# RWKV-7 attention with a mixture of experts on one core: from the ninth unit on, K and B are turned to channels on VectorE

## The chip, the cores and the metric

The kernel runs on one core of a Trainium2 chip. A core has TensorE (PE; its weight loads are listed as PEld), VectorE (DVE), ScalarE (ACT), GpSimd (POOL) and SyncE (SP), which here only issues DMAs. Each engine works through its own instructions in order and waits at semaphores for the others. The metric is device time in microseconds (us) of one execution; of several runs, the median.

## The reference

Attention over 4 batches, 8 heads, 768 tokens and a head dimension of 40, with a state that decays channel by channel, and then four expert networks, weighted per token:

```python
for t in range(S):                                     # attention, S = 768
    kt, vt, rt = (k[:, :, t], v[:, :, t], r[:, :, t])
    wt, at, bt = (w[:, :, t], a[:, :, t], b[:, :, t])
    y[:, :, t] = np.einsum('bhd,bhde->bhe', rt, state)
    Sa = np.einsum('bhde,bhe->bhd', state, at)
    state_decay = state * wt[:, :, None, :] - np.einsum('bhd,bhe->bhde', Sa, bt)
    state = state_decay + np.einsum('bhd,bhe->bhde', vt, kt)
...
p = domain_probs / (domain_probs.sum(-1, keepdims=True) + 1e-09)
for e in range(E):                                     # mixture, E = 4, F = 1024
    h = np.maximum(x @ w1[e], 0.0)
    out += p[:, e:e + 1] * (h @ w2[e])
```

All data is float32.

## The kernel before

**Units and passes.** The 768 tokens are cut into 12 chunks of 64, and the 4 batches into 2 pairs. A unit is one chunk of one pair: 24 units, `u = 2 * chunk + pair`. The main loop (L1221) makes a pass for each unit. In pass u the generator `within` (L462) prepares unit u + 2, `substitute` (L638) solves its triangular system, `merge` (L704) joins the two halves of the solution of unit u + 1, and `step` (L742) brings the state forward by a unit. Between these parts, pieces of the mixture (`mix`, L1088) of earlier chunks fill TensorE. From unit 7 on (`q.apart`) the order is always the same.

**Layouts.** "By channels" is a tile with channels on the partitions: 128 partitions are two halves of 64 (heads of one parity), of which 40 rows hold channels, and the free side holds 8 blocks of 64 tokens. "By tokens" has the 64 tokens of two batches on the partitions and 8 heads of 40 (padded to 64) on the free side. `load` (L239) brings W, B, K and V by tokens, two DMAs each. `load_raw` (L247) brings W, A, R and V in pieces that VectorE's 32x32 transpose (`turn_raw`, L284) makes into the layout by channels: four DMAs for W or A, eight for R or V.

**Decay.** In `within`, VectorE turns raw W into G (L470) and makes a running product over the tokens by a scan (L511), with `first` marking where each block starts over. G holds the product before each token; `gl` is the product over all 64. TensorE then turns G to tokens (pg, four transposes of 128x128, L525), VectorE multiplies by W (gp, L528) and takes the reciprocal (L529), and N = -B/gp and K/gp are made by tokens (L556, L561). TensorE turns N and K to channels (pNT, pKT, four transposes each), and ScalarE copies them from PSUM (L535). A is turned by VectorE and multiplied by G (AT, L565). N and K by tokens are used again by `step`, in pdy; NT and KT by channels give pf and pe, the products with AT.

**Substitution.** F is the copy of pf. `substitute` copies its diagonal blocks (`blocks`, L643: VectorE two of them, ScalarE two), turns them (M, L651), makes Z1 and Z2 on VectorE (L663, L667), and then GpSimd runs a chain of 48 multiplications and additions over Z (L681, L698). In the next pass `merge` turns Z into Qc and QTc on VectorE (L709, L710), and TensorE multiplies with QTc (pY). Then come prn, RH (L760) and the rest of the step.

**Mixture.** A chunk of two units has 256 tokens. ph is x @ w1, hs its Relu (L888); sums of halves of hs (a, L1014) and of w2 replace one product in eight; p is the product with w2, which VectorE adds to the output (osb, L903).

**What sets the order.** TensorE's order is the program's. On VectorE, a scheduler puts the instructions in order before the run; a list written out by hand (`VECTOR_ORDER`) binds the order up to unit 7's reciprocal. SP's DMAs are issued in order, and the list `later` (L1083) holds moves that are begun three or six at a time behind pieces of the mixture. In a pass the copies of Y to xT (L854, 12 DMAs) stand in the same queue.

Of the kernel before, what the change touches and what calls it, by code (L numbers as in the profile page):

```python
# [33 lines left out]
def kernel(  # L34
# [87 lines left out]
    def of_mixture(name):  # L122
        return ps.tile([P, 512], FP32, name=name, tag="mm", bufs=3)
# [49 lines left out]
                        base=(2 * j + s) * D - g * P, channel_multiplier=1,  # L173
                    )

    first = const.tile([P, 2 * NJ, L], FP32, name="first")
    nc.gpsimd.memset(first[:], 0.0)
    nc.gpsimd.memset(first[:, :, 0:1], 1.0)


    def kept(name, shape, n, value=0.0, eng=nc.gpsimd, lo=0):
        tiles = []
        for i in range(n):
            t = const.tile(shape, FP32, name=f"{name}{i}")
# [12 lines left out]


    PADDED = 3
    padded = {}  # L200
    for n, a_sum in enumerate(("a1", "a7", "a5", "a2")):
        t = padded["RV"[n % 2], n // 2] = sb.tile([P, H, 64], FP32, name="padded", tag=a_sum)
        nc.gpsimd.memset(t[:, :, D:64], 0.0)
    raw = {x: kept(f"raw{x}", [P, 2 * NJ, 2 * D], 1, 0.0, nc.vector, D + D - Q) for x in "WARV"}
    k_tok, n_tok = (kept(x, of_64, 2, lo=D) for x in ("k_tok", "n_tok"))

    both = [P, H, D + L]
# [19 lines left out]
    units = []  # L227
# [10 lines left out]

    def load(q, names):  # L239
        for x in names:  # L240
            q.n[x] = t = sb.tile([P, H, D], FP32, name=f"nat{x}", tag=f"nat{x}", bufs=2 if x in "WV" else 1)
            for i, bb in enumerate(q.b):
                nc.sync.dma_start(
                    out=t[i * L:(i + 1) * L], in_=srcs[x][bb, :, q.c * L:(q.c + 1) * L, :].rearrange("h t e -> t h e"),
                )
# [27 lines left out]
    def part(i):  # L273
        return slice(i * L, (i + 1) * L)
# [119 lines left out]
    def half(s):  # L394
        return slice(64 * s, 64 * s + 64)
# [8 lines left out]
    def by(x, n):  # L404
        return x.rearrange("p (h e) -> p h e", e=n)
# [56 lines left out]
    def within(q):  # L462
# [3 lines left out]
        def pin(ins, also=False):  # L466
            if q.u <= PADDED or also:
                keep(ins)


        G = sb.tile([P, 2 * NJ * L + 1], FP32, name="G", tag="G", bufs=3)
        q.G = Gv = G[:, 0:2 * NJ * L].rearrange("p (c t) -> p c t", t=L)
        ahead = G[:, 1:2 * NJ * L + 1].rearrange("p (j i t) -> p i j t", i=2, t=L)
        for i in range(2):
            pin(noted(turn_raw(ahead[:, i], n["rawW"][:, NJ * i:NJ * i + NJ, :]), "G", q.u, i), q.u > EARLY + 2)
        q.gl = sb.tile([P, 2 * NJ, 1], FP32, name="gl", tag="gl", bufs=4)
        ins = nc.vector.tensor_tensor(out=q.gl[:], in0=G[:, L::L][:, :, None], in1=first[:, :, 0:1], op=ALU.mult)
        pin(noted(ins, "gl", q.u))
        pin(noted(nc.vector.memset(Gv[:, :, 0:1], 0.0), "G0", q.u))
        q.AT = sb.tile([P, 2 * NJ, L], FP32, name="AT", tag="AT", bufs=2)  # L480

# [24 lines left out]
        if q.u == 1:  # L506
            yield
            VT = turn_rv("V")
            yield
            turn_rv("R")  # L510
            yield  # L511
        ins = nc.vector.tensor_tensor_scan(
            out=G[:, 0:2 * NJ * L], data0=G[:, 0:2 * NJ * L],
            data1=first[:].rearrange("p c i -> p (c i)"), initial=0.0, op0=ALU.mult, op1=ALU.add,
        )
        pin(noted(ins, "scan", q.u))
        ins = nc.vector.tensor_tensor(out=q.gl[:], in0=q.gl[:], in1=Gv[:, :, L - 1:L], op=ALU.mult)
        noted(ins, "gll", q.u)
        if q.u == 1:
            yield  # L520
        if q.u < 3:
            pin(noted(turn_raw(q.AT[:], n["rawA"][:]), "AT", q.u))
        yield

        pg = turn("pg", tok(Gv), q.u == 2, of_mixture("pg") if q.u == 1 else None)  # L525
        pg = by(pg[:], 64)[:, :, 0:D]
        gp = sb.tile([P, H, D], FP32, name="gp")
        pin(noted(nc.vector.tensor_tensor(out=gp[:], in0=pg, in1=n["W"][:], op=ALU.mult), "gp", q.u))  # L528
        pin(noted(nc.vector.reciprocal(out=gp[:], in_=gp[:]), "1/gp", q.u))  # L529

        yield

        def turned(name, x):
            t = sb.tile([P, NJ, P], FP32, name=name, tag="turned", bufs=3)
            nc.scalar.copy(out=t[:].rearrange("p j t -> p (j t)"), in_=turn("p" + name, tok(x), q.u == 1)[:])  # L535
            return t

        def token_V():
            return n["paddedV"][:, :, 0:D] if q.u < PADDED else n["V"][:]

        def causal_scores(VT):
            pc = quadrants(banks("pc"), 0, BY_TOKENS, L, lambda j, s, i: (
                d_half(j, s), i, j, of_slots(VT, d_half(j, s), j, i, D), of_slots(q.RT, d_half(j, s), j, i, D),
            ))
            if q.u == 0:
                return pc
            masks(pc)

        def masks(pc):
# [6 lines left out]
        ins = nc.vector.scalar_tensor_tensor(  # L556
            out=q.N[:, :, 0:D], in0=n["B"][:], scalar=-1.0, in1=gp[:], op0=ALU.mult, op1=ALU.mult,
        )
        pin(noted(ins, "N", q.u))
        other = nc.gpsimd if q.u == 1 else nc.vector  # L560
        pin(noted(other.tensor_tensor(out=q.K[:, :, 0:D], in0=n["K"][:], in1=gp[:], op=ALU.mult), "K", q.u))  # L561
        if q.u > 2:
            pin(noted(turn_raw(q.AT[:], n["rawA"][:]), "AT", q.u))
        at_ij = q.AT[:].rearrange("p (i j) t -> p i j t", i=2)
# [6 lines left out]
            VT = turn_rv()  # L571
        yield

        NT = turned("NT", q.N)
        KT = turned("KT", q.K)
        if q.u == 2:
            VT = turn_rv()
        yield

        if q.u == 1 or q.u >= PADDED:  # L580
            causal_scores(VT)
            yield

        p = banks("pfe")
        pf = quadrants(p, 0, BY_TOKENS, L, lambda j, s, i: (
            s, i ^ s, j, of_slots(q.AT, s, j, i), of_pairs(NT, s, j, i),
        ))
        def copy_F():
            q.F = sb.tile([P, H, L], FP32, name="F", tag="F", bufs=1)
# [6 lines left out]
        if q.apart or q.u == 0:  # L596
            p = banks("pe")
        pe = quadrants(p, NJ * L, BY_TOKENS, L, lambda j, s, i: (
            s, i, j, of_pairs(KT, s, j, i), of_slots(q.AT, s, j, i),
        ))  # L600
        if not q.apart:
            copy_F()
# [139 lines left out]
    def step(q, xT):  # L742
# [85 lines left out]
        if not q.start:  # L828
            noted(nc.vector.tensor_tensor(out=Y[:], in0=Y[:], in1=Gv, op=ALU.mult), "YG", q.u)
        if not q.end:  # L830
            gl = q.gl[:].rearrange("p (j i) o -> p j i o", i=2)
# [389 lines left out]
    for u in range(1, NU):  # L1221
# [56 lines left out]
        if u + 3 < NU:  # L1278
            if u == 1:
                go_now(load_raw(begin(4), "WVRA"))  # L1280
            else:
                go(load_raw(units[u + 3] if ahead else begin(u + 3), "A" if ahead else "WA"))
            load(units[u + 3], "WBKV")
            if u > 1:
                later.extend(load_raw(units[u + 3], "VR"))
        run(w, 2)
# [86 lines left out]
```

## Time and profile before

| | us |
|---|---|
| median of 3 runs | 1081.11 |
| lowest and highest run | 1079.75, 1083.7 |
| span of the profiled execution, first to last instruction | 1077.3 |
| GpSimd: Z additions (L698), 704 of them | 263.8 |
| GpSimd: Z multiplications (L681), 352 of them | 142.8 |
| VectorE: reciprocal (L529), 24 of 2.152 | 51.6 |
| VectorE: gp (L528), 24 of 0.477 | 11.4 |
| VectorE: transposes of raw W (L286), 48 of 0.436 | 20.9 |
| VectorE: N (L556) and K (L561) | 12.3, 13.3 |
| ScalarE: copies of NT and KT (L535) | 13.9, 14.4 |

The profile is one execution, taken by the hardware profiler. A row of its timeline has the start in us from the span's start, the duration of the group in us, engine, line, operation, the tile that is written and those that are read, the shape, and how many instructions are merged; a bracket shows how long the engine was idle before it and what it waited for. Matmuls overlap one another: durations of a group can reach into the next.

### The profile page before, as it was taken

The page shows a single profiled execution, that of the slowest core. Times are in us where ns is not written, and L with a number is a line of the kernel's source. Part 1 is how long each engine was busy: PE and PEld are TensorE (multiplying, and loading weights), DVE is VectorE, ACT ScalarE, POOL GpSimd, SP SyncE. Part 2 cuts the span into 40 slices and gives each one's busy share as a digit, 9 for nine tenths or more (in the row PEclk, how much of TensorE's full clock was granted, in tenths as well). Part 3 has the DMA queues.
Part 4 walks back from the last instruction along what each step waited for, and adds up shares of the span by engine and source line. Part 5 has one row for each costly group of instructions (what it writes and reads, how often), then busy time and mean ns, then how long its engine had stood idle before and what let it go on. Part 6 is the DMA issues. An engine that isn't in the chain of part 4 may idle for free.

```text
span 1077.3 us, 38510 instructions
## 1 busy us (share of the span) xinstructions
PE 1062.5 (99%) x16140; PEld 955.1 (89%) x16140; DVE 758.3 (70%) x1549; ACT 353.2 (33%) x958; POOL 494.3 (46%) x1276
## 2 busy tenths in 40 slices
PE   7999999999999999999999999999999999999998
PEld 7878878899898999999999999999999999998887
DVE  7787679897676776876776768668767776634343
ACT  3433444422432423324333333233243333221110
POOL 5117777747254374363462653733735626520000
PEclk9999999999999999999999999999999999999999
DMA  7776644444444434443353263353343331121220
GB/s 129 192 202 129 142 108 108 101 85 102 103 103 104 104 92 85 115 99 79 91 129 80 59 155 62 83 128 81 90 106 86 96 89 58 54 82 42 84 76 13
DMA packets 258070, 105.81 MB, mean 98 GB/s; under 512 B 212536, under 2 KB 237672, under 8 KB 257896
## 3 DMA queue, kind: packets, MB, share of 16 engines
q1 hardware_dynamic: 253912, 102.51, 40.8%
q8 instruction: 127, 2.08, 0.8%
q10 hardware_dynamic: 3984, 0.84, 0.5%
q14 instruction: 47, 0.39, 0.1%
HBM read 95.40 MB, written 3.93 MB: 92 GB/s over the span
## 4 chain that ended last, share of the span: by engine, by line
PE 93%; DVE 3%; DMA 1%; ACT 1%; issue 1%; SPq 0%; POOL 0%; ACTq 0%; DVEq 0%
PE ph L110 40%; PE p L110 31%; PE pdy L110 3%; PE po L110 3%; PE pxr L110 2%; PE psat L110 2%; PE prn L110 2%; PE pfe L110 2%; PE pc L110 1%; PE pev L110 1%; PE pQ L110 1%; PE pe L110 1%; PE pNT L113 1%; PE pg L113 1%; PE pKT L113 1%; PE pY L110 1%
## 5 line engine op out<-in xcount | busy, mean ns | idle before, releaser
L698 POOL TENSOR_TENSOR Z<-Z 128x31 f32<-128x31 f32 (+7 forms) x704 | 263.8, 375 | 55.2
L1014 DVE TENSOR_TENSOR a<-hs 128x512 f32<-128x512 f32 x220 | 150.7, 703 | 111.6 <-ACT hs L888 111.6
L110 PE MATMUL ph<-xT,w1a 128*128 128x256 f32 (+3 forms) x1536 | 221.3, 374 | 1.7 <-issue 1.7
L888 ACT ACTIVATE hs<-ph 128x512 f32<-128x512 f32 (+1 forms) x208 | 116.9, 564 | 323.5 <-PE ph L110 323.1
L110 PE MATMUL ph<-xT,w1b 128*128 128x256 f32 (+3 forms) x1536 | 222.0, 374 | 0.0
L110 PEld LDWEIGHTS ph<-xT,w1a 128*128 128x128 f32 (+1 forms) x1536 | 167.9, 161 | 30.6 <-issue 9.5
L110 PEld LDWEIGHTS ph<-xT,w1b 128*128 128x128 f32 (+1 forms) x1536 | 168.8, 161 | 26.9 <-issue 6.1
L681 POOL TENSOR_TENSOR Z<-M,Z 128x62 f32<-128x62 f32 (+7 forms) x352 | 142.8, 406 | 98.0 <-DVE M L667 72.1
L110 PE MATMUL p<-sums,a 128*128 128x160 f32 x1056 | 164.9, 299 | 0.0
L903 DVE SCALAR_TENSOR_TENSOR osb<-p,gate,osb 128x320 f32<-128x320 f32 (+1 forms) x243 | 108.1, 481 | 79.2 <-PE p L110 72.9
L110 PEld LDWEIGHTS p<-sums,a 128*128 128x128 f32 x1056 | 152.8, 190 | 2.2
L648 POOL COPY below<-F 32x256 f32<-32x256 f32 x48 | 21.4, 445 | 227.5 <-ACT F L591 225.8
L110 PEld LDWEIGHTS p<-w,hs 128*128 128x128 f32 x704 | 98.6, 190 | 8.5 <-issue 7.3
L110 PE MATMUL p<-w,hs 128*128 128x160 f32 x704 | 104.9, 302 | 0.0
L110 PE MATMUL p<-w,a 128*128 128x160 f32 x704 | 102.8, 299 | 0.0
L110 PEld LDWEIGHTS p<-w,a 128*128 128x128 f32 x704 | 98.0, 190 | 0.0
L716 POOL COPY QT<-QTc 32x256 f32<-32x256 f32 x96 | 40.3, 420 | 71.6 <-DVE QTc L710 65.3
L808 ACT COPY RS<-pxr 64x256 f32<-64x256 f32 x88 | 32.3, 367 | 101.2 <-DVE SX L460 78.8
L629 ACT COPY EV<-pev 64x160 f32<-64x160 f32 x96 | 23.1, 286 | 90.5 <-PE pev L110 90.1
L529 DVE RECIPROCAL gp<-gp 128x320 f32<-128x320 f32 x24 | 51.6, 2152 | 0.7
L651 DVE STREAM_TRANSPOSE M<-blocks 128x1024 f32<-128x1024 f32 x24 | 47.3, 1969 | 2.9 <-ACT blocks L643 2.8
L460 DVE COPY_PREDICATED VC<-mask_up,pc 128x256 f32<-128x256 int32 x48 | 18.7, 443 | 38.4 <-PE pc L110 38.4
(153 smaller groups left out, 1389.4 us busy)
## 6 DMA issues: line engine op xcount, KB each, us to landing
w1a<-in_moe_w_dram SPq DMA_DIRECT2D x37, 512.0 KB
w1b<-in_moe_w_dram SPq DMA_DIRECT2D x37, 512.0 KB
w<-in_moe_w_dram SPq DMA_DIRECT2D x4, 1280.0 KB
w1a<-in_moe_w_dram SPq DMA_DIRECT2D x74, 64.0 KB
w1b<-in_moe_w_dram SPq DMA_DIRECT2D x74, 64.0 KB
natW<-in_w_dram SPq DMA_DIRECT2D x48, 80.0 KB
natB<-in_b_dram SPq DMA_DIRECT2D x48, 80.0 KB
natK<-in_k_dram SPq DMA_DIRECT2D x48, 80.0 KB
```

Source lines behind the costliest of these rows:

```text
L110: return stated(nc.tensor.matmul(**k))
L113: return stated(nc.tensor.transpose(**k))
L529: pin(noted(nc.vector.reciprocal(out=gp[:], in_=gp[:]), "1/gp", q.u))
L629: nc.scalar.copy(out=of_slot(q.EV[half(p)], i ^ p)[:, :, 0:D], in_=pev[i][half(p)])
L651: ins = nc.vector.transpose(out=M[:], in_=cols)
L681: ins = eng.tensor_tensor(out=Z[:, 1:3, 0:n, j + 1:Q], in0=M[:, j:j + 2, None, j + 1:Q].to_broadcast([P, 2, n, m]), in1=Z[:, here, 0:n, j: ...
L698: eng.tensor_tensor(out=z[:, 0], in0=z[:, 0], in1=z[:, x], op=ALU.add)
L716: ins = nc.gpsimd.tensor_copy(out=q.QT[quarter(i), :, quarter(i % 2)], in_=QTc[quarter(i)])
L808: nc.scalar.copy(out=RS[half(s), x ^ s::2], in_=prs[x][half(s)].rearrange("p (j i) t -> p j i t", i=2),)
L888: ins = nc.scalar.activation(out=h[:, i * HF // 2:(i + 1) * HF // 2, 0:n], in_=ph[i][:], func=ACTF.Relu,)
L903: ins = nc.vector.scalar_tensor_tensor(out=to, in0=p, scalar=sc, in1=to, op0=ALU.mult, op1=ALU.add)
L1014: ins = nc.vector.tensor_tensor(out=t[:], in0=x, in1=y, op=op)
```

## The change

From unit 8 on (`BY_CHANNEL`), units are prepared by channels. G gets a column more in each block (65 instead of 64), so that `gl` is that column and needs no instructions of its own. The reciprocal is taken of G by channels (128x512), without pg and gp. Raw B and K are loaded instead of W, B and K by tokens, VectorE turns them (two transposes each) and multiplies them by the reciprocal; TensorE turns the results to tokens (pNT, pKT), and ScalarE copies them to N and K. pNT and pKT stand in front of pfe instead of in front of pc. The raw loads of B and K of a unit are put on the list `later` at the end of a pass, and so are begun in the next pass. In units before the ninth W, B and K by tokens lie in the buffers of raw B and K. The products with NT, KT and AT read 40 rows of each half instead of 64 in all units.

```diff
+    BY_CHANNEL = 8
...
+        by_channel = q.u >= BY_CHANNEL
+        G = sb.tile([P, 2 * NJ, L + 1], FP32, name="G", tag="G", bufs=3)
+        flat = G[:].rearrange("p c t -> p (c t)")
+        if by_channel:
+            q.G = Gv = G[:, :, 0:L]
+            ahead = G[:, :, 1:L + 1].rearrange("p (j i) t -> p i j t", i=2)
...
+        if by_channel:
+            q.gl = G[:, :, L:L + 1]
...
+        if q.u == BY_CHANNEL:
+            set_starts(L + 1)
...
-        pg = turn("pg", tok(Gv), q.u == 2, of_mixture("pg") if q.u == 1 else None)
-        pg = by(pg[:], 64)[:, :, 0:D]
-        gp = sb.tile([P, H, D], FP32, name="gp")
-        pin(noted(nc.vector.tensor_tensor(out=gp[:], in0=pg, in1=n["W"][:], op=ALU.mult), "gp", q.u))
-        pin(noted(nc.vector.reciprocal(out=gp[:], in_=gp[:]), "1/gp", q.u))
+        gp = sb.tile([P, 2 * NJ, L], FP32, name="gp")
+        if by_channel:
+            pin(noted(nc.vector.reciprocal(out=gp[:], in_=G[:, :, 1:L + 1]), "1/gp", q.u))
+        else:
...
+        def to_tokens(name, x, to):
+            p = turn("p" + name, tok(x))
+            nc.scalar.copy(out=to[:, :, 0:D], in_=by(p[:], 64)[:, :, 0:D])
...
-        NT = turned("NT", q.N)
-        KT = turned("KT", q.K)
+        if not by_channel:
+            NT = turned("NT", q.N)
+            KT = turned("KT", q.K)
...
             causal_scores(VT)
+            if by_channel:
+                NT = sb.tile([P, 2 * NJ, L], FP32, name="NT", tag="turned", bufs=3)
+                KT = sb.tile([P, 2 * NJ, L], FP32, name="KT", tag="turned", bufs=3)
+                for t, x in ((NT, "B"), (KT, "K")):
+                    for i in range(2):
+                        turn_raw(t[:, i::2], n["raw" + x][:, NJ * i:NJ * i + NJ])
+                    if x == "B":
+                        nc.vector.scalar_tensor_tensor(
+                            out=t[:], in0=t[:], scalar=-1.0, in1=gp[:], op0=ALU.mult, op1=ALU.mult,
+                        )
+                    else:
+                        nc.vector.tensor_tensor(out=t[:], in0=t[:], in1=gp[:], op=ALU.mult)
             yield
+        if by_channel:
+            to_tokens("NT", NT, q.N)
+            to_tokens("KT", KT, q.K)
...
-            load(units[u + 3], "WBKV")
+            load(units[u + 3], "V" if u + 3 >= BY_CHANNEL else "WBKV")
...
             begin_later(len(later))
             gap(3)
+        if BY_CHANNEL <= u + 3 < NU:
+            if u + 3 == BY_CHANNEL:
+                pad_raw()
+            later.extend(load_raw(units[u + 3], "BK"))
```

`set_starts` writes `first` anew for blocks of 65 and `pad_raw` clears the padding of raw B and K: four memsets on GpSimd, once.

In the changed program's order of instructions, VectorE has in each of these passes: the state's update, then B's transposes and product (NTm is the product), then Qc, QTc, VC, RH, the next unit's G and scan, K's transposes and product, the next unit's reciprocal, and then the mixture's a sums and blocks. SP has the last two of K's four loads right behind the 12 copies of Y to xT.

More of the change, by code (lines that the diff above doesn't have):

```diff
@@ L174, in set_pick, with starts_of, set_starts @@
                     )
-    first = const.tile([P, 2 * NJ, L], FP32, name="first")
-    nc.gpsimd.memset(first[:], 0.0)
-    nc.gpsimd.memset(first[:, :, 0:1], 1.0)
+    first = const.tile([P, 2 * NJ, L + 1], FP32, name="first")
+    def starts_of(width):
+        return first[:].rearrange("p c t -> p (c t)")[:, 0:2 * NJ * width].rearrange("p (c t) -> p c t", t=width)
+    def set_starts(width):
+        nc.gpsimd.memset(first[:], 0.0)
+        nc.gpsimd.memset(starts_of(width)[:, :, 0:1], 1.0)
+    set_starts(L)
     def kept(name, shape, n, value=0.0, eng=nc.gpsimd, lo=0):
@@ L203, with by_tokens, pad_raw @@
         nc.gpsimd.memset(t[:, :, D:64], 0.0)
-    raw = {x: kept(f"raw{x}", [P, 2 * NJ, 2 * D], 1, 0.0, nc.vector, D + D - Q) for x in "WARV"}
+    PAD = D + D - Q
+    raw = {x: kept(f"raw{x}", [P, 2 * NJ, 2 * D], 1, float(x == "W"), nc.vector, PAD) for x in "WARV"}
+    room = {x: const.tile([P, 2 * NJ, 2 * D], FP32, name=f"raw{x}") for x in "BK"}
+    raw.update((x, lambda t=t: t) for x, t in room.items())
+    def by_tokens(x, u):
+        at = {"B": ("B", 0), "K": ("K", 0), "W": ("BK"[u % 2], NJ)}[x]
+        flat = room[at[0]][:, at[1]:at[1] + NJ, :].rearrange("p n e -> p (n e)")
+        return flat.rearrange("p (h e) -> p h e", e=D)
+    def pad_raw():
+        for x in "BK":
+            nc.gpsimd.memset(room[x][:, :, PAD:2 * D], 0.0)
     k_tok, n_tok = (kept(x, of_64, 2, lo=D) for x in ("k_tok", "n_tok"))
@@ L240, in load @@
         for x in names:
-            q.n[x] = t = sb.tile([P, H, D], FP32, name=f"nat{x}", tag=f"nat{x}", bufs=2 if x in "WV" else 1)
+            if x == "V":
+                t = sb.tile([P, H, D], FP32, name="natV", tag="natV", bufs=2)[:]
+            else:
+                t = by_tokens(x, q.u)
+            q.n[x] = t
             for i, bb in enumerate(q.b):
@@ L421, in of_pairs @@
     def of_pairs(x, hf, j, i):
-        return x[half(hf), j, part(i)]
+        return x[64 * hf:64 * hf + D, 2 * j + i, :]
     def of_slots(x, hf, j, i, n=64):
@@ L468, in pin @@
                 keep(ins)
-        G = sb.tile([P, 2 * NJ * L + 1], FP32, name="G", tag="G", bufs=3)
-        q.G = Gv = G[:, 0:2 * NJ * L].rearrange("p (c t) -> p c t", t=L)
-        ahead = G[:, 1:2 * NJ * L + 1].rearrange("p (j i t) -> p i j t", i=2, t=L)
+        by_channel = q.u >= BY_CHANNEL
[5 more added lines that the diff above has]
+        else:
+            q.G = Gv = flat[:, 0:2 * NJ * L].rearrange("p (c t) -> p c t", t=L)
+            ahead = flat[:, 1:2 * NJ * L + 1].rearrange("p (j i t) -> p i j t", i=2, t=L)
         for i in range(2):
             pin(noted(turn_raw(ahead[:, i], n["rawW"][:, NJ * i:NJ * i + NJ, :]), "G", q.u, i), q.u > EARLY + 2)
-        q.gl = sb.tile([P, 2 * NJ, 1], FP32, name="gl", tag="gl", bufs=4)
-        ins = nc.vector.tensor_tensor(out=q.gl[:], in0=G[:, L::L][:, :, None], in1=first[:, :, 0:1], op=ALU.mult)
-        pin(noted(ins, "gl", q.u))
+        if by_channel:
+            q.gl = G[:, :, L:L + 1]
+        else:
+            q.gl = sb.tile([P, 2 * NJ, 1], FP32, name="gl", tag="gl", bufs=3)[:]
+            ins = nc.vector.tensor_tensor(
+                out=q.gl, in0=flat[:, L:2 * NJ * L + 1:L][:, :, None], in1=starts_of(L)[:, :, 0:1], op=ALU.mult,
+            )
+            pin(noted(ins, "gl", q.u))
         pin(noted(nc.vector.memset(Gv[:, :, 0:1], 0.0), "G0", q.u))
@@ L511, in within @@
             yield
+        if q.u == BY_CHANNEL:
+            set_starts(L + 1)
+        decays = flat if by_channel else flat[:, 0:2 * NJ * L]
+        starts = starts_of(L + 1 if by_channel else L)
         ins = nc.vector.tensor_tensor_scan(
-            out=G[:, 0:2 * NJ * L], data0=G[:, 0:2 * NJ * L],
-            data1=first[:].rearrange("p c i -> p (c i)"), initial=0.0, op0=ALU.mult, op1=ALU.add,
+            out=decays, data0=decays, data1=starts.rearrange("p c t -> p (c t)"), initial=0.0, op0=ALU.mult,
+            op1=ALU.add,
         )
         pin(noted(ins, "scan", q.u))
-        ins = nc.vector.tensor_tensor(out=q.gl[:], in0=q.gl[:], in1=Gv[:, :, L - 1:L], op=ALU.mult)
-        noted(ins, "gll", q.u)
+        if not by_channel:
+            ins = nc.vector.tensor_tensor(out=q.gl, in0=q.gl, in1=Gv[:, :, L - 1:L], op=ALU.mult)
+            noted(ins, "gll", q.u)
         if q.u == 1:
@@ L523, in within @@
         yield
-        pg = turn("pg", tok(Gv), q.u == 2, of_mixture("pg") if q.u == 1 else None)
-        pg = by(pg[:], 64)[:, :, 0:D]
-        gp = sb.tile([P, H, D], FP32, name="gp")
-        pin(noted(nc.vector.tensor_tensor(out=gp[:], in0=pg, in1=n["W"][:], op=ALU.mult), "gp", q.u))
-        pin(noted(nc.vector.reciprocal(out=gp[:], in_=gp[:]), "1/gp", q.u))
+        gp = sb.tile([P, 2 * NJ, L], FP32, name="gp")
+        if by_channel:
+            pin(noted(nc.vector.reciprocal(out=gp[:], in_=G[:, :, 1:L + 1]), "1/gp", q.u))
+        else:
+            pg = turn("pg", tok(Gv), q.u == 2, of_mixture("pg") if q.u == 1 else None)
+            pg = by(pg[:], 64)[:, :, 0:D]
+            gp = gp[:].rearrange("p c t -> p (c t)")[:, 0:H * D].rearrange("p (h e) -> p h e", e=D)
+            pin(noted(nc.vector.tensor_tensor(out=gp, in0=pg, in1=n["W"], op=ALU.mult), "gp", q.u))
+            pin(noted(nc.vector.reciprocal(out=gp, in_=gp), "1/gp", q.u))
         yield
         def turned(name, x):
-            t = sb.tile([P, NJ, P], FP32, name=name, tag="turned", bufs=3)
-            nc.scalar.copy(out=t[:].rearrange("p j t -> p (j t)"), in_=turn("p" + name, tok(x), q.u == 1)[:])
-            return t
+            t = sb.tile([P, 2 * NJ, L], FP32, name=name, tag="turned", bufs=3)
+            nc.scalar.copy(out=t[:].rearrange("p c t -> p (c t)"), in_=turn("p" + name, tok(x), q.u == 1)[:])
+            return t
+        def to_tokens(name, x, to):
+            p = turn("p" + name, tok(x))
+            nc.scalar.copy(out=to[:, :, 0:D], in_=by(p[:], 64)[:, :, 0:D])
         def token_V():
-            return n["paddedV"][:, :, 0:D] if q.u < PADDED else n["V"][:]
+            return n["paddedV"][:, :, 0:D] if q.u < PADDED else n["V"]
         def causal_scores(VT):
@@ L555, in within @@
         q.K, q.N = k_tok(), n_tok()
[L556 to L559, printed above, removed]
         other = nc.gpsimd if q.u == 1 else nc.vector
-        pin(noted(other.tensor_tensor(out=q.K[:, :, 0:D], in0=n["K"][:], in1=gp[:], op=ALU.mult), "K", q.u))
+        if not by_channel:
+            ins = nc.vector.scalar_tensor_tensor(
+                out=q.N[:, :, 0:D], in0=n["B"], scalar=-1.0, in1=gp, op0=ALU.mult, op1=ALU.mult,
+            )
+            pin(noted(ins, "N", q.u))
+            pin(noted(other.tensor_tensor(out=q.K[:, :, 0:D], in0=n["K"], in1=gp, op=ALU.mult), "K", q.u))
         if q.u > 2:
@@ L572, in within @@
         yield
-        NT = turned("NT", q.N)
-        KT = turned("KT", q.K)
+        if not by_channel:
+            NT = turned("NT", q.N)
+            KT = turned("KT", q.K)
         if q.u == 2:
@@ L581, in within @@
             causal_scores(VT)
+            if by_channel:
[7 more added lines that the diff above has]
+                            out=t[:], in0=t[:], scalar=-1.0, in1=gp[:], op0=ALU.mult, op1=ALU.mult,
+                        )
+                    else:
+                        nc.vector.tensor_tensor(out=t[:], in0=t[:], in1=gp[:], op=ALU.mult)
             yield
+        if by_channel:
+            to_tokens("NT", NT, q.N)
+            to_tokens("KT", KT, q.K)
         p = banks("pfe")
         pf = quadrants(p, 0, BY_TOKENS, L, lambda j, s, i: (
-            s, i ^ s, j, of_slots(q.AT, s, j, i), of_pairs(NT, s, j, i),
+            s, i ^ s, j, of_slots(q.AT, s, j, i, D), of_pairs(NT, s, j, i),
         ))
@@ L598, in within @@
         pe = quadrants(p, NJ * L, BY_TOKENS, L, lambda j, s, i: (
-            s, i, j, of_pairs(KT, s, j, i), of_slots(q.AT, s, j, i),
+            s, i, j, of_pairs(KT, s, j, i), of_slots(q.AT, s, j, i, D),
         ))
@@ L830, in step @@
         if not q.end:
-            gl = q.gl[:].rearrange("p (j i) o -> p j i o", i=2)
+            gl = q.gl.rearrange("p (j i) o -> p j i o", i=2)
             for i in range(2):
```

## The prediction

> **What bounds the kernel now.** I read the page first: busy time, then the chain of waits.
>
> ```profile
> PE 1062.5 (99%) x16140; PEld 955.1 (89%) x16140; DVE 758.3 (70%) x1549; ACT 353.2 (33%) x958; POOL 494.3 (46%) x1276
> ...
> PE 93%; DVE 3%; DMA 1%; ACT 1%; issue 1%; SPq 0%; POOL 0%; ACTq 0%; DVEq 0%
> ```
>
> TensorE is busy for 99% of the span and holds 93% of the chain. The view of busy time in stretches of 45 us shows it at 45.00 of 45.00 from 360 us to 1035 us. So work taken from TensorE after unit 7 shortens the kernel, as long as TensorE never has to wait for another engine. How near the others are is read in the timelines of one pass. I take the pass from one pfe product (582.67 us) to the next (625.09 us): 42.42 us. TensorE first:
>
> ```profile
> 601.28 1.25 PE L110 MATMUL p<-sums,a 128*128 128x160 f32 x8
> 602.37 0.60 PE L113 MATMUL pg<-ident,G 128*128 128x128 f32 x4
> 602.90 0.68 PE L110 MATMUL pev<-VC,ET 64*64 64x40 f32 x32
> ...
> 612.78 0.60 PE L113 MATMUL pNT<-ident,n_tok 128*128 128x128 f32 x4
> ...
> 613.75 0.69 PE L110 MATMUL pc<-RT,VT 40*64 40x64 f32 x32
> 614.27 0.57 PE L110 MATMUL pY<-QTc,below 64*64 64x64 f32 x13
> ...
> 625.09 0.69 PE L110 MATMUL pfe<-NT,AT 64*64 64x64 f32 x32
> ```
>
> Then VectorE (DVE) in the same pass; a bracket is the idle time before an instruction, and what ended it:
>
> ```profile
> 608.51 0.48 DVE L556 SCALAR_TENSOR_TENSOR n_tok<-natB,gp 128x320 f32<-128x320 f32 x1
> ...
> 611.82 0.45 DVE L710 STREAM_TRANSPOSE QTc<-Qc 128x256 f32<-128x256 f32 x1
> 614.52 0.78 DVE L460 COPY_PREDICATED VC<-mask_up,pc 128x256 f32<-128x256 int32 x2 [2.26 <-PE pc L110]
> ...
> 616.07 0.51 DVE L760 TENSOR_TENSOR RH<-prn,EV 128x160 f32<-128x160 f32 x2
> ...
> 621.48 1.29 DVE L1014 TENSOR_TENSOR a<-hs 128x512 f32<-128x512 f32 x2 [1.66 <-ACT hs L888]
> ...
> 626.57 0.69 DVE L643 COPY blocks<-F 32x256 f32<-32x256 f32 x2
> ```
>
> GpSimd's (POOL) substitution closes a loop: blocks, M, Z1, Z2 on DVE, then a 21.7 us chain on POOL (588.71 to the last pair, below), then Qc and QTc on DVE, then pY on TensorE:
>
> ```profile
> 609.91 0.52 POOL L698 TENSOR_TENSOR Z<-Z 128x8 f32<-128x8 f32 x2
> ```
>
> It ends at 610.43, Qc runs at 611.17, QTc ends at 612.27, pY needs it at 614.27. The slack of this loop is 0.74 + 2.00 us. The last view is the DMA queue that SyncE (SP) feeds:
>
> ```profile
> 650.47 8.91 SPq L854 DMA_DIRECT2D xT<-Y  x12
> 659.49 1.44 SPq L243 DMA_DIRECT2D natB<-in_b_dram  x2
> ```
>
> The 12 copies of Y to xT hold the queue for 9.02 us (650.47 to 659.49), beginning where Y*G ends on DVE.
>
> **The change part by part.**
>
> *TensorE, removed.* Units 8 to 23 lose the four pg transposes, in passes 6 to 21. From pg's start to pev is 0.53 us. Products before a 64-row group take 0.09 us longer than before a 128-row one (sums to pfe 1.18 us, 623.91 to 625.09; sums to pg 1.09 us), and that now falls on pev. Gain 0.53 - 0.09 = 0.44 us a pass, 16 passes: -7.0 us. The four pNT and four pKT stay in number. They move from before pc to before pfe (0.97 us, 612.78 to 613.75): no gain, but pc, pY and RH now stand 0.97 us nearer to the pfe before them.
>
> The Trainium skill speaks for more: "TensorE: Matmul & The Clock Gate", Part 4: PE-mode transpose, gives about 275 ns for one 128x128 transpose in a kernel. The trace has 272 ns as the duration of one too, but four in a row take 0.53 us because they overlap. By the page's figure the gain would be an estimated 16 x 4 x 0.275 = 17.6 us; the measurement decides.
>
> *VectorE, off the path.* gp (0.48) and its reciprocal (2.15) no longer stand before Y, nor N and K between the state updates; B's two transposes (0.44 each) and its product (0.62 from start to start) follow the state. Y now starts when pdy is there. pdy's last matmul ends at 605.17 (604.92 + 0.25), 0.44 us earlier in the new pass, and 0.08 us passes before DVE starts (as from pc to VC): 604.81. Y*G ends 1.53 us later (564.10 to 565.63 in the pass before), 606.34. That is 1.7 us sooner than now (608.04), and gains nothing, since TensorE never waited there.
>
> *VectorE, on the path.* pc and pY stand at 612.34 and 612.87 (0.44 + 0.97 earlier). RH can start some 1.15 us after pY (estimated: prn's products for RH end 1.07 us after pY's start, plus 0.08), 614.02. Then, from starts in the timeline: RH 0.44, G 0.93, scan 1.26; done at 616.65. Next in the built order stand K's transposes, K's product, and only then the reciprocal of the following unit, before the mixture's a sums. The reciprocal over 512 elements, by the rows for 24 (0.289 us) and 320 (2.152 us), is an estimated 3.36 us, 3.28 from start to start.
>
> *The wait added.* K's last two raw loads are issued behind the 12 xT copies in every pass (the built order of SP). xT starts at 606.34 and ends at 615.36; the last K load starts 0.5 us later. How long it takes to land has no row. Nearest: rawV's last load starts at 630.66 and VT starts at 632.84 after a wait of 1.84 us that the view puts down to this queue's raw loads: 2.2 us. Low bound 1.05 us (rawR's packets begin that long after their issue), high bound 3 us. I take 2.2, the row of a wait of the same kind: K is there at 618.06, and DVE stands 1.4 us. Queued behind it: K's product, the reciprocal, five a sums, the osb updates, blocks. Then 0.92 + 0.62 + 3.28 = 622.88; the a sums and osb updates 4.62 us (579.06 to 584.15 less the 0.47 idle in it): 627.50. The changed order lets AT and AT*G (1.24) stand before blocks in every second pass, with VT (0.64) before Z2; in the others AT stands in idle time before RH, or (three of them, each after a stall) between blocks and M.
>
> The next pfe is at 625.09 - 0.44 = 624.65. So blocks stands 2.85 us after it in one kind of pass, 4.09 in the other, against 1.48 now. With VT, Z2 is late by 1.2 us in one, 3.2 in the other (2.61 + 0.64). POOL's chain is as long as before, since N's product keeps two SBUF inputs in it, while K's leaves it.
>
> The skill has a rule here ("SBUF — State Buffer", Who interferes with whom): a DVE instruction with two SBUF inputs and a GpSimd one exclude each other. The trace agrees with it: a pair of POOL additions takes 1.51 us where a sums run beside it, 0.74 just before. By it K's product outside the chain would give back at most its own estimated 0.6 us a pass.
>
> *Where the lateness goes.* In the late kind, POOL ends at 613.6, QTc at 614.8 (0.08 + 0.65 + 0.45), pY starts at 614.9 and not at 612.87: TensorE stands 2.0 us. In every second such case NTm stands between Qc and QTc (0.62): 2.3 on average. In the other kind QTc ends at 612.8, and a pass that follows a stall starts with that much slack: no stall. A stall of ph on the osb updates (they free its PSUM bank an estimated 0.9 us after ph wants it) falls in the same late pass and is part of this time, since pY waits for DVE and POOL either way. Passes 7 to 21 are 15, so 7.5 late ones x 2.2 = +16.5 us.
>
> Sum: -7.0 + 16.5 = +9.5 on the profiled span of 1077.3: 1086.8. The runs' median, 1081.1, stands 3.8 above that span, so 1090.6; I say 1090.
>
> SP's issues (eight raw loads for six plain ones) have gaps of us before each weight piece and cost nothing; without that gap, two issues are 0.9 us a pass. The scan's 520 elements cost 0.02 us. POOL's four memsets come once, inside a chain: 1.2 us at most (0.52 and 0.11 for `first` at the start, 0.27 for each memset of 256 columns on DVE).
>
> **The rivals.**
> 1. *No change.* K lands at the low bound, 1.2 us sooner. Late passes then cost 1.0 us: -7.0 + 7.5 = +0.5, 1081.6, and 1077 to 1086 with half a microsecond more or less in each. For: DVE is idle 3 us twice in each pass. Against: these stand behind Z2, too late for blocks.
> 2. *Faster.* POOL's loop keeps its 2.7 us of slack and TensorE loses only pg: 1081.1 - 7.0 = 1074. It needs Z2 late by less than 1.3 us in every pass (0.74 + 2.00 less the 1.41 by which pY comes nearer). For: DVE is at 70%. Against: the reciprocal alone, 3.28, on a path with 1.66 us idle.
> 3. *Worse: every pass stalls.* K lands at 3 us and both kinds run over: +0.8 in each of 15, -7.0 + 16.5 + 12 = 1103; half of it, 1096.
>
> **How the numbers follow.** Forecast 0.53 (1086 to 1095), rival 1 0.22, rival 2 0.14, rival 3 0.11. 0.5% of the time (5.4 us) is what a measurement can tell from no change: 1075.7 to 1086.5. Faster 0.15, same 0.24, slower 0.61. The range reaches into rivals 1 and 3: 1077 to 1099.
>
> **What would show it.** In the profile after: no pg from pass 6 on; KT waiting for rawK, 1 to 2 us in each pass; pY waiting for QTc about 2 us in every second pass; GpSimd's wait for M longer by 1 to 3 us. If KT waits for nothing, the load's landing was mis-sized; if TensorE stays at 45.00 of 45.00, POOL's loop had more room and rival 2 holds.

## The result, and the profile after

The changed kernel takes 1094.51 us (median of 4 runs, 1092.04 to 1096.11) against 1081.97 for the kernel before (1079.75 to 1083.7): a ratio of 1.0117, 95% interval 1.0093 to 1.014. It is slower, by some 12.5 us; the forecast was 1090.0, the range 1077 to 1099. The profiled execution has a span of 1093.8 us against 1077.3; that is one execution of each kernel, and these two lie 16.4 us apart where the medians lie 12.5.

From the page of the changed kernel, the busy times and the chain that ended last:

```profile
PE 1065.2 (97%) x16076; PEld 954.3 (87%) x16076; DVE 798.6 (73%) x1565; ACT 351.6 (32%) x958; POOL 506.3 (46%) x1280
...
PE 45%; POOL 25%; DVE 14%; SPq 6%; issue 6%; DMA 2%; ACT 1%; DVEq 0%; ACTq 0%; POOLq 0%
```

TensorE held 93% of the chain before and holds 45% now. What came in is the loop of blocks, GpSimd's substitution and QTc (POOL 25%, DVE 14%) and SyncE's queue (6%). The waits of the changed kernel between 330 and 1090 us (waiting tile, what it waited for, total us, times, longest) name the places:

```profile
DVE Qc L775 <- POOL Z L764: 22.9, 14, 3.1
...
DVE KT L311 <- DMA rawK<-in_k_dram: 15.3, 11, 2.6
...
PE pY L110 <- DVE QTc L776: 9.6, 11, 1.9
```

KT waits 11 times for raw K, 1.4 us on average; Qc waits 14 times for GpSimd, and pY 11 times for QTc. GpSimd's wait for M is 4.6 us a pass (69.7 in 15) against 3.4 before (51.3 in 15). One case can be followed from end to end. The timeline of the changed kernel, first the queue of SP:

```profile
444.57 7.54 SPq L920 DMA_DIRECT2D xT<-Y  x10
452.16 1.18 SPq L289 DMA_DIRECT2D rawK<-in_k_dram  x2
```

Then VectorE, from there to the next pass:

```profile
451.93 1.24 DVE L552 TENSOR_TENSOR_SCAN G<-G,first 128x520 f32<-128x520 f32 x1
455.73 0.77 DVE L311 STREAM_TRANSPOSE KT<-rawK 128x256 f32<-128x256 f32 x2 [2.56 <-DMA rawK<-in_k_dram]
456.54 0.69 DVE L644 TENSOR_TENSOR KT<-KT,gp 128x512 f32<-128x512 f32 x1
457.27 3.35 DVE L568 RECIPROCAL gp<-G 128x512 f32<-128x512 f32 x1
...
465.34 0.57 DVE L709 COPY blocks<-F 32x256 f32<-32x256 f32 x2
...
469.89 0.69 DVE L733 TENSOR_TENSOR M<-M,Z 128x512 f32<-128x512 f32 x1
...
492.58 0.61 DVE L775 STREAM_TRANSPOSE Qc<-Z 128x256 f32<-128x256 f32 x1 [3.07 <-POOL Z L764]
```

And TensorE:

```profile
493.82 0.59 PE L110 MATMUL pY<-QTc,below 64*64 64x64 f32 x13 [1.86 <-DVE QTc L776]
```

K's last loads are issued when xT's copies leave the queue (452.1), KT starts at 455.73 after a wait of 2.56, and the reciprocal follows it. blocks starts 4.66 us after this pass's pfe (460.68), where it stood at 1.48 before; Z2 (the last M) at 9.21 instead of 5.21. GpSimd ends 4.1 us later (31.9 us after pfe instead of 27.8), and TensorE, which never stood in this place in the kernel before (from 240 us on), stands 1.86 us. That is the path of the prediction's middle part, a little beyond its late kind (Z2 4.0 us late here, 3.2 there).

The kernel before had 45.00 busy us of TensorE in every 45 from 360 to 1035 us. The same view of the changed kernel, three neighbouring stretches and a short one inside the third (columns: stretch, its length, busy us of PE, PEld, DVE, ACT and POOL, the granted TensorE clock, DMA share, GB/s):

```profile
405.00:450.00 45.00, 44.77 (x722) 40.98 (x726) 34.00 (x67) 14.68 (x41) 22.33 (x59) 0.96 0.38 83
450.00:495.00 45.00, 42.95 (x685) 38.73 (x680) 33.64 (x64) 14.44 (x40) 21.32 (x55) 1.00 0.40 100
495.00:540.00 45.00, 45.00 (x717) 40.80 (x710) 34.99 (x68) 15.38 (x44) 21.70 (x57) 0.96 0.36 81
495.20:498.60 3.40, 3.40 (x48) 2.75 (x38) 2.98 (x7) 1.51 (x6) 0.33 (x1) 0.50 0.45 83
```

The second has 2.05 us of TensorE idle. The first and the third show something that the busy time hides: the granted clock is 0.96, because TensorE ran at half clock for 3.4 us (the last line) shortly after a wait of pY.

Pass by pass, from pfe to pfe, the time is found in these places:

| | us |
|---|---|
| 16 passes with new work, at their length without any stall: 41.99 instead of 42.42 | -6.9 |
| passes from 286.21 to 938.08 (15): 651.87 us less 15 x 41.99 | +22.0 |
| kernel before, its own stall in the pass from 325.62 (44.74) and small change, gone | -2.5 |
| the first changed pass, from 241.88: 44.33 (42.52 before) beyond the shorter pass | +2.2 |
| up to the first changed pass (241.88 against 240.69) and behind the last | +1.5 |
| sum, before rounding | +16.4 |

The spans differ by as much. Of the 22.0, the delay of pY against pc makes 13.5 (it should start 0.52 us after pc; it is late in 13 of 15 passes, by 0.2 to 2.0), the delay of pc makes 4.9 (the products before it stood earlier in the pass), and the two half-clock stretches of 3.4 us some 3.4. The 1.2 of the early part isn't shown to be the change's: the kernels of the experiments below reach this pass anywhere from 240.88 to 243.01, and that of experiment 4, which is the kernel before up to there, starts the pass ahead of it 2.3 us later than the kernel before did (192.57 against 190.31).

pc's delay has a source that the traces show. In each of the five passes with pc late by over 0.3 us, the third product of ph starts 0.10 or 0.11 us after an osb update ends on VectorE. The largest case, 1.9 us, is in the pass from 850.77; VectorE first, then TensorE:

```profile
845.13 0.77 DVE L311 STREAM_TRANSPOSE KT<-rawK 128x256 f32<-128x256 f32 x2 [1.87 <-DMA rawK<-in_k_dram]
...
852.73 0.38 DVE L969 SCALAR_TENSOR_TENSOR osb<-p,minus_gate,osb 128x160 f32<-128x160 f32 x1
```

```profile
853.21 0.87 PE L110 MATMUL ph<-xT,w1a 64*64 64x256 f32 x11 [1.32 <-issue]
```

The profile names no releaser for this wait. The interval of 0.10 or 0.11 also comes back in experiments 1, 2 and 6, so the osb update is taken as the cause. VectorE comes to it late, because it stands behind the reciprocal.

### The profile page after: what moved, and what is told of

The parts are those of the page before. It is cut to its first block, busy times and chain, and to the rows that moved or that the text cites. A ratio compares the mean times of both kernels' runs of the same rounds, so it can differ in the third digit from the quotient of the medians.

```text
span 1093.8 us, 38502 instructions
## 1 busy us (share of the span) xinstructions
PE 1065.2 (97%) x16076; PEld 954.3 (87%) x16076; DVE 798.6 (73%) x1565; ACT 351.6 (32%) x958; POOL 506.3 (46%) x1280
## 4 chain that ended last, share of the span: by engine, by line
PE 45%; POOL 25%; DVE 14%; SPq 6%; issue 6%; DMA 2%; ACT 1%; DVEq 0%; ACTq 0%; POOLq 0%
PE ph L110 20%; POOL Z L764 16%; PE p L110 14%; POOL Z L747 9%; SPq L920 3%; DVE M L717 3%; SPq L289 2%; DVE a L1080 2%; PE po L110 2%; PE prn L110 1%; DVE gp L568 1%; DVE osb L969 1%; PE psat L110 1%; PE pdy L110 1%; DVE M L733 1%
## 5 line engine op out<-in xcount | busy, mean ns | idle before, releaser
L764 POOL TENSOR_TENSOR Z<-Z 128x31 f32<-128x31 f32 (+7 forms) x704 | 252.0, 358 | 55.1
L110 PE MATMUL ph<-xT,w1a 128*128 128x256 f32 (+3 forms) x1536 | 223.7, 377 | 1.7 <-issue 1.7
L110 PE MATMUL ph<-xT,w1b 128*128 128x256 f32 (+3 forms) x1536 | 224.6, 377 | 0.7 <-issue 0.7
L1080 DVE TENSOR_TENSOR a<-hs 128x512 f32<-128x512 f32 x220 | 155.3, 725 | 87.6 <-ACT hs L954 87.6
L747 POOL TENSOR_TENSOR Z<-M,Z 128x62 f32<-128x62 f32 (+7 forms) x352 | 152.9, 434 | 119.0 <-DVE M L733 93.2
L714 POOL COPY below<-F 32x256 f32<-32x256 f32 x48 | 31.2, 649 | 218.8 <-ACT F L657 217.2
L568 DVE RECIPROCAL gp<-G 128x512 f32<-128x512 f32 x16 | 53.6, 3353 | 0.5
L775 DVE STREAM_TRANSPOSE Qc<-Z 128x256 f32<-128x256 f32 x24 | 15.0, 625 | 38.7 <-POOL Z L764 38.5
```

The source lines that it names most:

```text
L110: return stated(nc.tensor.matmul(**k))
L568: pin(noted(nc.vector.reciprocal(out=gp[:], in_=G[:, :, 1:L + 1]), "1/gp", q.u))
L714: tc.keep_in_program_order(nc.gpsimd.tensor_copy(out=q.below[quarter(i)], in_=q.F[quarter(i), :, 0:Q]))
L747: ins = eng.tensor_tensor(out=Z[:, 1:3, 0:n, j + 1:Q], in0=M[:, j:j + 2, None, j + 1:Q].to_broadcast([P, 2, n, m]), in1=Z[:, here, 0:n, j: ...
L764: eng.tensor_tensor(out=z[:, 0], in0=z[:, 0], in1=z[:, x], op=ALU.add)
L1080: ins = nc.vector.tensor_tensor(out=t[:], in0=x, in1=y, op=op)
```

## Experiments

In the first expectations A is the prediction's reading, that VectorE is late by K's wait and by the reciprocal together, and B that K's landing alone decides; the other letters are rivals of these two. Ratios are against the kernel before, run on the same chip beside each group.

**1. K's loads ahead of the copies.** All raw loads that are still on the list are begun before the copies of Y to xT; in the traces those that move are K's last two. Nothing else is changed in the program, but the scheduler then gives K's work another place on VectorE (below).

```diff
             run(w_next)
+            begin_later(len(later))
             run(s)
```

> The changed kernel with one edit: all raw loads still on the list are begun in front of the copies of Y to xT, so that K's last two loads no longer stand behind them. Theory A (VectorE's work between RH and blocks is late by K's wait AND by the reciprocal, and GpSimd's loop hands that on to pY): KT's wait for rawK falls from 15 us to under 2, pY's wait falls to less than half, time 1079 to 1087 (ratio to before 0.998 to 1.005). Rival B (K's landing alone): all of the loss goes, 1074 to 1077 (0.993 to 0.996). Rival C (the reciprocal's place alone): no better than the changed kernel, 1091 to 1096.

Measured: 1075.3 us (1073.16 to 1078.32), ratio 0.9946 [0.9928, 0.9964]. The whole loss is gone, and the kernel is faster than before. The expected time of A was too high; B's was met. The timeline of this kernel in the pass from 370.07, SP:

```profile
389.63 1.93 SPq L289 DMA_DIRECT2D rawK<-in_k_dram  x4
393.72 8.91 SPq L920 DMA_DIRECT2D xT<-Y  x12
```

And VectorE:

```profile
399.43 0.45 DVE L776 STREAM_TRANSPOSE QTc<-Qc 128x256 f32<-128x256 f32 x1
399.80 0.73 DVE L311 STREAM_TRANSPOSE KT<-rawK 128x256 f32<-128x256 f32 x2
400.56 0.82 DVE L644 TENSOR_TENSOR KT<-KT,gp 128x512 f32<-128x512 f32 x1
401.31 0.77 DVE L485 COPY_PREDICATED VC<-mask_up,pc 128x256 f32<-128x256 int32 x2
402.04 0.56 DVE L826 TENSOR_TENSOR RH<-prn,EV 128x160 f32<-128x160 f32 x2
...
404.59 3.35 DVE L568 RECIPROCAL gp<-G 128x512 f32<-128x512 f32 x1
...
413.54 0.69 DVE L709 COPY blocks<-F 32x256 f32<-32x256 f32 x2
```

Not only the wait is gone. With K there early, its transposes and product (1.5 us) stand between QTc and VC, in time in which VectorE had been waiting for pc. So the stretch behind RH is shorter by the wait and by K's own work, some 2.9 us, and the reciprocal now fits: blocks starts 1.48 us after the next pfe (412.06), as in the kernel before. K's work has this place in every second pass. In the others, that from 412.06 for one, it stands between VC and RH, and RH starts 0.6 to 1.2 us later than in the first kind (31.97 us after pfe). Of the 16 passes 14 take 41.98 to 42.16 us, with blocks 1.48 to 2.37 us after pfe, so TensorE hardly stands in them.

**2. and 3. The reciprocal back in front of Y.** With the changed kernel's loads (2) and with those of experiment 1 (3), the reciprocal is bound to its old place between the mixture's a sums and Y.

```diff
-            pin(noted(nc.vector.reciprocal(out=gp[:], in_=G[:, :, 1:L + 1]), "1/gp", q.u))
+            pin(noted(nc.vector.reciprocal(out=gp[:], in_=G[:, :, 1:L + 1]), "1/gp", q.u), True)
```

> The changed kernel with one edit: the reciprocal is kept in the program's order, which puts it before Y, as in the kernel before, and out of the way of the a sums and blocks. Theory A: the path from RH to blocks loses 3.3 us, but Y, and with it the copies to xT and K's last loads, come about 2 us later, so KT's wait grows to 3 us or more a pass and eats half of it: 1082 to 1091. Rival B (K's landing alone): worse than the changed kernel, 1096 or more. Rival C (the reciprocal's place alone): 1074 to 1077.

Measured: 1090.4 us (1086.65 to 1092.29), ratio 1.008 [1.006, 1.0099]. This is in A's range; B and C missed. In the passes from 285.75 us on, Y starts 24.95 us after pfe on average, where it was 22.35 in the changed kernel, and KT waits 2.8 us for raw K instead of 1.05 (means of 15 passes): what the reciprocal's place gives is eaten by the later copies, as A said.

> Both edits together. Theory A: blocks at most 1.5 us after pfe as in the kernel before, no wait of pY, and the four pg transposes of 16 units are gained: 1074 to 1077 (0.993 to 0.996). Rivals B and C say the same. Rival D (the changed products, transposes or port contention cost time by themselves, whatever is late): 1083 or more.

Measured: 1084.4 us (1082.99 to 1085.65), ratio 1.0032 [1.0023, 1.0041]. A, B and C had expected 7 to 10 us less. Only D's bound of 1083 and above was met, but not for D's reason: experiment 1 has the same products and transposes and takes 1075.3. Together with experiment 1 it makes a square:

| median, us | reciprocal behind the scan | reciprocal before Y |
|---|---|---|
| K's last loads behind xT | 1094.5 | 1090.4 |
| K's loads ahead of xT | 1075.3 | 1084.4 |

K's loads cost 19.2 in one column and 6.0 in the other. And with K early, the old place of the reciprocal is the worse one by 9.1. With K late it is the better one by about 4; the intervals of these two ratios overlap a little (1.0093 and 1.0099), so that size is uncertain. The timeline of experiment 3 says why the old place is worse with K early, VectorE first:

```profile
605.54 3.34 DVE L568 RECIPROCAL gp<-G 128x512 f32<-128x512 f32 x1
608.80 0.69 DVE L889 TENSOR_TENSOR Y<-pdy,RS 128x256 f32<-128x256 f32 x2
...
611.59 0.77 DVE L311 STREAM_TRANSPOSE NT<-rawB 128x256 f32<-128x256 f32 x2
...
613.75 0.62 DVE L775 STREAM_TRANSPOSE Qc<-Z 128x256 f32<-128x256 f32 x1
...
614.82 0.41 DVE L776 STREAM_TRANSPOSE QTc<-Qc 128x256 f32<-128x256 f32 x1
```

Then TensorE:

```profile
615.37 0.59 PE L110 MATMUL pY<-QTc,below 64*64 64x64 f32 x13 [0.63 <-DVE QTc L776]
```

pdy is done before the reciprocal is: Y starts at 608.80, right behind it, and no bracket stands on any line up to QTc, so VectorE itself is late here, not GpSimd (its chain ended at 613.07, before Qc). In the kernel before, the same order had room:

```profile
603.93 0.48 DVE L528 TENSOR_TENSOR gp<-pg,natW 128x320 f32<-128x320 f32 x1
604.45 2.15 DVE L529 RECIPROCAL gp<-gp 128x320 f32<-128x320 f32 x1
606.52 0.69 DVE L823 TENSOR_TENSOR Y<-pdy,RS 128x256 f32<-128x256 f32 x2
```

From gp's start to QTc's end (612.27) it took 8.34 us there; from the reciprocal's start to QTc's end it takes 9.69 here. The reciprocal alone takes 3.26 us up to Y's start, where gp and reciprocal together took 2.59. The rest up to QTc's end is 0.7 longer, with B's transposes and product in it instead of N and K by tokens. With a start 0.3 us later, QTc ends 31.24 us after pfe instead of 29.60. And pY stands at 30.27 where nothing holds it up (experiment 1), instead of 31.59. So 2.0 us of room became a lateness of 1.0. This was read from the traces; the parts were not tried one by one.

**4. The gain by itself.** The kernel before, without the pg transposes from unit 8 on. gp is then W times W, so the decay inside a chunk is left out of N and K there.

```diff
-        pg = turn("pg", tok(Gv), q.u == 2, of_mixture("pg") if q.u == 1 else None)
-        pg = by(pg[:], 64)[:, :, 0:D]
+        if q.u < 8:
+            pg = turn("pg", tok(Gv), q.u == 2, of_mixture("pg") if q.u == 1 else None)
+            pg = by(pg[:], 64)[:, :, 0:D]
+        else:
+            pg = n["W"][:]
```

> The kernel before without the four pg transposes of units 8 to 23 (gp is then W times W, so the decay is left out of N and K there). Theory A: TensorE's gain alone, 0.44 us in 16 passes: 1074 (0.9935, 0.992 to 0.995). By 0.275 us for each transpose it would be 1063 to 1065. If pg was hidden, 1081.

Measured: 1074.92 us (1073.36 to 1077.14), ratio 0.9945 [0.9929, 0.996], against 1081.22 for the kernel before in this group: 6.3 us less. A pass takes 41.97 to 42.02 us from 373.74 us on, instead of 42.40 to 42.55. The row of the trace (0.44 a pass) was right. The 17.6 us that the prediction worked out from the Trainium skill's "TensorE: Matmul & The Clock Gate", Part 4: PE-mode transpose, are not seen.

**5. The first reciprocal by channels alone.** Experiment 1 with unit 8's reciprocal, the one in the pass ahead of the first changed one, in its old place.

```diff
-            pin(noted(nc.vector.reciprocal(out=gp[:], in_=G[:, :, 1:L + 1]), "1/gp", q.u))
+            pin(noted(nc.vector.reciprocal(out=gp[:], in_=G[:, :, 1:L + 1]), "1/gp", q.u), q.u == BY_CHANNEL)
```

> x1_k_early with one thing more: the first reciprocal by channels (unit 8's, in the pass that starts near 190 us) is bound to stand before Y, as in before; the others stay behind the scan. In x1 the passes from 286 us on take 41.98 to 42.10 us (one of 43.28), but the first one with VectorE's new work, from 241.66, takes 44.34, with blocks 4.20 us after pfe; in x3, where this reciprocal stood before Y, it takes 42.94 and blocks stand at 2.10. Theory: unit 8's reciprocal alone makes that pass late, so the span falls by 1.4 us: 1073 to 1075 against x1's 1075.3 in the median, that pass 42.5 to 43.0. Rival (that pass is late by something else, the raw loads that come new in it): no change, 44.3.

Measured: 1073.43 us (1073.22 to 1075.05), ratio 0.9937 [0.9925, 0.995]. The pass from 243.01 takes 42.94 us, where experiment 1 had 44.34, with blocks 2.10 us after pfe instead of 4.20: as the theory says. Against experiment 1 the ratios alone would not tell it (their intervals overlap); the pass does. By the median this version is the fastest of all here.

**6. and 7. VectorE made late without any DMA.** Experiment 1 with an extra reciprocal just ahead of the real one, of 192 elements (6) or 448 (7), which the real one overwrites.

```diff
         if by_channel:
+            if q.u > BY_CHANNEL:
+                nc.vector.reciprocal(out=gp[:, 0:3], in_=G[:, 0:3, 1:L + 1])
             pin(noted(nc.vector.reciprocal(out=gp[:], in_=G[:, :, 1:L + 1]), "1/gp", q.u))
```

(7 has `0:7` in both places.)

> x1_k_early with a reciprocal of 192 elements ahead of each reciprocal from unit 9 on, into the same tile, which the full one then overwrites: some 1.3 us more of VectorE on the path from scan to blocks (worked out from 0.289 us for 24 and 3.353 for 512), with no DMA wait. Theory L (only the length of VectorE's stretch between RH and blocks counts, wherever it comes from): x1 has 0.8 to 1.5 us of room (Qc to QTc end at 28.5 to 29.7, pY at 30.27 after pfe), so stalls of 0 to 0.5 us in 15 passes: 1075 to 1083. Rival Q (it is the queue: x1 gains because raw K no longer competes with xT and the weight pieces, not because VectorE is done sooner): no change, 1074 to 1076.5.

> As x6, with 448 elements: some 2.9 us more of VectorE between scan and blocks, which is what the changed kernel has more than x1 (1.4 of K's wait and 1.54 of K's transposes and product). Theory L: as the changed kernel, 1088 to 1100, with pY waiting 0.5 to 2 us in most passes. Rival Q: 1074 to 1077. Between the two, 1078 to 1087, would say that the wait for K's loads costs by more than its length.

Measured: 1084.86 us (1083.97 to 1085.43), ratio 1.0037 [1.0024, 1.0051], and 1106.06 us (1104.8 to 1107.32), ratio 1.0234 [1.022, 1.0248]. The extra reciprocals take 1.35 and 2.95 us. Q falls: the time goes up with K's loads as early as in experiment 1. L holds in kind, and both results lie above its ranges: 1.9 us over the upper end in 6, 6.1 in 7. The waits of TensorE in 7 between 240 and 940 us:

```profile
PE pY L110 <- DVE QTc L778: 21.2, 14, 2.1
```

And its busy time in two stretches of 45 us:

```profile
675.00:720.00 45.00, 43.20 (x662) 39.44 (x661) 36.26 (x67) 13.68 (x37) 21.72 (x55) 0.96 0.36 85
720.00:765.00 45.00, 44.51 (x676) 40.58 (x676) 37.51 (x66) 15.65 (x44) 22.82 (x55) 1.00 0.40 101
```

pY waits 1.5 us on average; and the granted clock of 0.96 comes back, four half-clock stretches in all, some 1.7 us each, about 7 of the 30.8 us that 7 takes more than experiment 1. Nearly all the rest is pY's lateness against pc: it sums to 23.0 in the 15 passes from 285.22 us, against 0.4 in experiment 1. Experiment 6 has no half-clock stretch. Of its 9.6 us, pY's lateness against pc makes 7.6 (8.0 against 0.4) and pc's own 2.0 (3.4 against 1.3).

The 2.9 us of experiment 7 cost 30.8, while K's late loads, which also put up to 2.9 us into the stretch, cost 19.2. Part of this is read from the traces. The extra reciprocal is there in each pass, but K's wait vanishes where a stall has made RH late (none in three of the 15 passes, 1.05 on average). And 7 has four half-clock stretches where the changed kernel has two.

**8. K's loads behind nine of the twelve copies.** The changed kernel with its last raw loads begun from inside the copies' loop:

```diff
                     nc.sync.dma_start(
                         out=xT[to:to + hi - lo, g, :],
                         in_=Y[at:at + hi - lo, h // 2].rearrange("p i t -> p (i t)"),
                     )
+                    copies.append(q.u)
+                    if q.u >= EARLY and copies.count(q.u) == 9:
+                        begin_later(len(later))
```

> The changed kernel with K's last loads begun behind 9 of the 12 xT copies instead of behind all 12: K lands 2.25 us sooner (9.0 us for 12 copies), near 33.2 us after pfe, when VectorE has G and the scan done or nearly so. The wait of 1.4 us goes, K's 1.54 us of work stays behind RH. Theory L: half of the stretch's excess is left, as x6: 1075 to 1084. Theory that any load of K behind xT keeps the whole loss: 1090 to 1096. Theory that the wait was all: 1074 to 1077.

Measured: 1088.39 us (1085.99 to 1088.8), ratio 1.0072 [1.0057, 1.0087]: between two of the expectations and outside all three. Two lines of its VectorE timeline show what they left out:

```profile
405.80 0.77 DVE L311 STREAM_TRANSPOSE KT<-rawK 128x256 f32<-128x256 f32 x2 [3.17 <-DMA rawK<-in_k_dram]
406.49 0.29 DVE L826 TENSOR_TENSOR RH<-prn,EV 128x160 f32<-128x160 f32 x1
```

The scheduler, which lays VectorE's order down before the run, put KT ahead of the scan in every second pass (8 of 16), and in four of these ahead of one of the two RH instructions or of both. In the case shown the loads (issued from 401.76 to 402.77) were not there until 405.8, so the wait moved in front of RH instead of going away. In the other passes KT stands behind the scan, as in the changed kernel. So the experiment changed two things, and its time gives no clean price for the wait alone.

## Why the prediction was right, point by point

The path was right, and its sign; the size was under-estimated: the sum has +9.5 us on the profiled span, and +16.4 came. The result, 1094.5, lies in the forecast's own stretch (1086 to 1095) near its upper end, and between the forecast and rival 3.

- *pg's gain, -7.0.* Right: -6.9 from the length of a pass without stalls, 0.43 to 0.44 each, and -6.3 in experiment 4.
- *The reciprocal, an estimated 3.36 us.* Right: 3.353 for 512 elements.
- *K behind the xT copies, DVE standing 1.4 us.* Right in kind and in mean (15.3 us in 11 waits), though not in each pass: where pY has stood, RH is late as well and K's wait gets shorter. Its landing was mis-sized: 2.2 us had been taken, with 3 as the high bound. Where KT waited for it, KT starts 2.0 to 3.6 us after the last load does, 2.75 on average (3.04 in the case shown first).
- *Z2 late by 1.2 or 3.2 us.* The mean over the 15 passes is 7.65 us after pfe, 2.4 late, against 2.2 predicted.
- *Stalls in every second pass, 2.2 each, 16.5.* Right in direction and sign, and mis-sized. From 373 to 593 us pY is late by 1.9, 0, 2.0, 0, 1.9: the alternation as predicted. In the other ten passes there is none: pY is late by 1.8 and 1.0 in the first two, and by 0.2 to 0.9 in each from 593 on. The prediction's second kind of pass had 0.06 us to spare (QTc at 612.8, pY at 612.87), so a landing half a microsecond longer is enough to make it late too: that is rival 3's condition in part. pY's lateness sums to 13.5. That this comes near 16.5 is partly luck, since 13 of 15 passes share it and not 7.5. But the prediction counted the delay of ph as part of the same time, and it came on top (4.9), as did the half clock (3.4), which it didn't foresee. Gross 22.0 where it said 16.5; net of the kernel before's own 2.5, 19.5. Two small steps of the sum don't close either: it works out 2.3 us for a late pass and multiplies by 2.2, and it has Z2 late by 1.2 us where its blocks is late by 1.37 (2.85 less 1.48).
- *The first changed pass.* Not in the sum: unit 8's reciprocal already stands behind the scan in the pass before, and the first changed pass is 2.2 too long. Experiment 5 takes 1.4 of its 44.34 us away by moving that reciprocal alone.
- *Y sooner "gains nothing".* True of the kernel before, misleading for the changed one: with a longer reciprocal, B to turn and pY nearer, the old place of the reciprocal costs 9.1 us (experiment 3 against 1). Moving it was worth having; this step of the prediction priced it at nothing.
- *Rival 2's condition, Z2 late by less than 1.3 us.* It marks the point well. In experiment 1 Z2 stands 5.58 to 6.29 us after pfe in the passes without a stall (0.4 to 1.1 late). In experiment 6 the passes with Z2 at 6.35 to 6.42 have none either, and those at 6.59 to 7.74 do.
- *"The reciprocal alone, 3.28, on a path with 1.66 us idle"*, the argument against rival 2, was too strong. With K there early the stretch is K's 1.5 us of work shorter as well, and the reciprocal fits. What decides is the sum of VectorE's time between RH and blocks, as experiments 6 and 7 show by adding to it: 1.3 us more cost 9.6, 2.9 more cost 30.8. K's queue place had put up to 2.9 us there.

What stays open: how much the 1.5 us of K's work and the 1.4 us of its wait would each cost alone (experiment 8 didn't separate them), and why the stalls alternate up to 593 us and are small in each pass behind it.

## What to carry to other kernels

A transfer that is hidden by its size can be late by its place in the queue: look at what is issued ahead of it, and when, before counting a load as free. When work is taken from the bounding engine, the other engines' deadlines move nearer by as much, so the room of every loop has to be read again in the new pass; here 2.7 us became 1.3 to 1.4. And an instruction's best place depends on what else is late: the same reciprocal gained some 4 us by standing before Y with K late and lost 9.1 with K early.

## What the chip showed that was not expected

A short stall of TensorE can cost twice. In the changed kernel and in experiments 4 and 7 the granted clock fell to half for single stretches of 3.4 us, at full work. In the changed kernel they begin at 406.46 and 495.21, that is 88.75 us or 26 x 3.413 apart; in experiment 7 at 582.21, 715.33, 804.07 and 892.82, 39, 26 and 26 such stretches apart; in experiment 4 there is one, at 288.79. Cut into a grid of that length, TensorE's timelines show what goes with them: all seven follow a stretch with 1.65 to 1.86 us of TensorE idle, and in the ten traces here, between 240 and 950 us, none follows one with 1.53 or less. Where the stall falls in the grid matters: in the kernel before and in experiment 4, TensorE stands for 1.74 us behind a pfe. In experiment 4 all of it lies in one stretch, and the clock falls (the pass takes 45.92 us). In the kernel before 1.53 of it lies in one, and the clock stays (the pass from 325.62 takes 44.74). A stall of 1.71 us that fell across two stretches in the changed kernel (in the pass from 549.18) cost no clock either. The Trainium skill, "TensorE: Matmul & The Clock Gate", Part 1: The HAM clock gate, has a free-running window of 3413 ns, which agrees with the spacing; it lets the clock fall after an idle window, and here a window about half idle was enough.
